# Converting 64-bit weights with a scaled float copy and a sign factor, and spreading the routing of a fused attention and expert kernel over three steps

## The chip, the cores and the metric

The kernel runs on one core of a Trainium2 chip. Its engines are TensorE (PE), VectorE (DVE), ScalarE (ACT), GpSimd (POOL) and SyncE (SP), which here only issues DMAs. Each engine runs its own instructions in the order in which they were issued, and waits on semaphores for the others. The metric is device time in microseconds (us), lower is better.

## The reference

Three layers follow one another:

```python
def phi(x):                                   # q, k, v: 4 x 8 heads x 576 x 64
    proj = x @ w_phi                          # 64 -> 128
    proj = proj - max(abs(proj), axis=-1)
    return concat([exp(proj), exp(-proj)])
kv = phi(k).T @ v;  z = phi(k).sum(tokens)
attn = (phi(q) @ kv) / (phi(q) @ z + 1e-6)    # 2304 tokens x 512
logits = attn @ w_gate                        # 8 experts
e = argmax(logits);  g = softmax(logits)[e]
y = g * (relu(attn @ w1[e]) @ w2[e])          # in order of tokens, up to 576 rows an expert
h = y @ w_in                                  # 512 -> 2048
out = (h - tanh(h)) @ w_out                   # 2048 -> 512
```

All inputs are float32, apart from `w_in` and `w_out`, which arrive as 64-bit floats (the division by sqrt makes them so) and are converted on the chip.

## The kernel before, in words

The first 235 us are attention, routing and weight conversion together; then come the experts and the last layer, unit by unit, almost wholly matmuls.

**Attention** runs in steps `s` over 18 chunks of 128 tokens (`for s in range(NCH + LAG + 2)`). A step works on the keys of chunk `s`, the queries of chunk `s - 5` (`proj("q", j)`) and the numerators of chunk `s - 6` (`num`). TensorE's order in a step: project the keys (L301), transpose the older queries (L377), sum key features times values of the chunk before (L343), project the queries (L301), numerators (L415), gates (L330). Both projections go through the same PSUM tile `xb`, so each of them waits until VectorE has read out the other one: `sub` takes a maximum (L309) and subtracts it (L312). A step is here reckoned from the start of its key projection to that of the next: step 9 begins at 65.89 us, step 18, the first without keys, at 171.84 us.

**Conversion.** A weight is two 32-bit words, `lo` and `hi`. Steps 5 to 17 convert one piece each of 128 x 1024 weights (8 of `w_in`, 5 of `w_out`): `cv_load` fetches the raw piece (two buffers, 1 MB) two steps ahead, `cv_main` runs `cv_bits` on VectorE: three integer instructions put the float together (L86, L89, L92), a fourth (L95) makes a 0/1 mask from the square that ScalarE takes of `hi` (L102, `cv_mask`), and GpSimd multiplies by it (L97). A step later `cv_hi` (ScalarE, L272) rounds the result to the high part and `cv_lo` (GpSimd, L275) subtracts for the low part. Six more pieces of 512 columns (`late_bits`) are converted inside the first expert unit.

**Routing** goes by groups of three chunks. When a group's last numerators are there (its `since` is 0), `route1` runs 14 short VectorE instructions (L443 to L484): gates, argmax, softmax weight. A step later TensorE counts ranks (`prefix`, L504 to L507) and VectorE runs `route2` and `table` (L516 to L560). Another step later TensorE adds the group to the slot table (`map_mm`, L578) and VectorE adds it up (`map_add`, L585). For the first three groups ScalarE then scales one chunk per step (`xscale`, L436) and SyncE stores it; for the others GpSimd scales all three at once (L491). `weave` deals these short instructions out on VectorE behind the query's `sub`.

What sets the order is the order of the calls in the step loop; each engine keeps it.

Of the kernel before, what the change touches and what calls it, by code (L numbers as in the profile page):

```python
# [8 lines left out]
F32 = mybir.dt.float32  # L9
F32R = mybir.dt.float32r  # L10
BF16 = mybir.dt.bfloat16
I32 = mybir.dt.int32
AF = mybir.ActivationFunctionType
ALU = mybir.AluOpType
AX = mybir.AxisListType

P = 128
# [20 lines left out]
def build(nc, tc, ctx, qT, kT, vT, v, w_phi, w_gate, w12, win, wout, out, cap):  # L38
# [7 lines left out]
    const = ctx.enter_context(tc.tile_pool(name="const", bufs=1))  # L46
# [13 lines left out]
    ident = const.tile([P, P], F32, name="ident")  # L60
    reg1 = const.tile([1, 1], I32, name="reg1")
    reg = const.tile([1, E], I32, name="reg")
    sq_b = const.tile([P, 2], F32, name="sq_b")
    ids = [const.tile([P, 6], I32, name=f"ids{i}") for i in range(2)]

    NS = 6 * U
    idt = const.tile([P, NS], mybir.dt.int16, name="idt")
    few = const.tile([P, 3 * E + 2], F32, name="few")
    srt, wu, uk, e1off = few[:, 0:E], few[:, E:2 * E], few[:, 2 * E:3 * E], few[:, 3 * E:]
    reg1f = e1off[:, 1:2]  # L70
# [10 lines left out]

    NP = 512

    def cv_bits(t, a, m):
        lo, hi = t[:, :, 0], t[:, :, 1]
        nc.vector.tensor_scalar(out=a, in0=hi, scalar1=3, scalar2=0x3FFFFFFF,  # L86
                                op0=ALU.logical_shift_left, op1=ALU.bitwise_and)
        yield
        nc.vector.scalar_tensor_tensor(out=a, in0=lo, scalar=29, in1=a,  # L89
                                       op0=ALU.logical_shift_right, op1=ALU.bitwise_or)  # L90
        yield
        nc.vector.scalar_tensor_tensor(out=a, in0=hi, scalar=-0x40000000, in1=a,  # L92
                                       op0=ALU.bitwise_and, op1=ALU.bitwise_or)
        yield
        nc.vector.tensor_scalar(out=m, in0=m, scalar1=1.0, scalar2=None, op0=ALU.is_ge)  # L95
        af = a.bitcast(F32)
        nc.gpsimd.tensor_tensor(out=af, in0=af, in1=m, op=ALU.mult)  # L97
        yield

    def cv_mask(t, m):  # L100

        nc.scalar.activation(out=m, in_=t[:, :, 1].bitcast(F32), func=AF.Square, scale=2.0 ** 15 / 1.125)  # L102

    def cv_split(af, fh, fl):
        nc.scalar.copy(fh, af)
# [21 lines left out]
    def attention():  # L127
# [14 lines left out]
        cv = stk.enter_context(tc.tile_pool(name="cv", bufs=2, side="right"))  # L142
# [35 lines left out]
            out=tri, in_=ones, compare_op=ALU.is_gt, fill=0.0, base=0,  # L178
# [70 lines left out]
        for src, dh, dl, n in ((win, w_in_h, w_in_l, 4 * FF2), (wout, w_oa_h, w_oa_l, NOA * DM)):  # L249
            fh = dh.rearrange("p a b -> p (a b)")  # L250
            fl = dl.rearrange("p a b -> p (a b)")
            for o in range(0, n, NPC):
                pieces.append((src, fh[:, o:o + NPC], fl[:, o:o + NPC], o))
        raw, cvw, cvm = {}, {}, {}
        NRAW = 2

        def cv_load(i):
            if i < len(pieces):
                raw[i] = cv.tile([P, NPC, 2], I32, tag="raw", name="raw", bufs=NRAW)
                cv_fetch(raw[i], pieces[i][0], pieces[i][3], NPC)  # L260

        def cv_m(i):
            cv_mask(raw.pop(i), cvm.pop(i))

        def cv_main(i):
            a = cv.tile([P, NPC], I32, tag="a", name="a")
            cvw[i] = a.bitcast(F32)
            cvm[i] = cv.tile([P, NPC], BF16, tag="m", name="m")
            yield from cv_bits(raw[i], a, cvm[i])

        def cv_hi(i):
            nc.scalar.copy(pieces[i][1], cvw[i])  # L272

        def cv_lo(i):
            nc.gpsimd.tensor_tensor(out=pieces[i][2], in0=cvw.pop(i), in1=pieces[i][1].bitcast(F32), op=ALU.subtract)  # L275
# [41 lines left out]
        def kexp(i):  # L317
            t = kd.pop(("k", i))
            e = kp_p.tile([P, H, 2, DF], F32, tag="kp", name="kp")
            nc.scalar.activation(out=e[:, :, 0, :], in_=t, func=AF.Exp)  # L320
            nc.scalar.activation(out=e[:, :, 1, :], in_=t, func=AF.Exp, scale=-1.0)
            kp[i] = e

# [65 lines left out]
        early = groups[:3]  # L389
        xq, late = [], []  # L390
        GM = max(map(len, groups))
        dls, rs, rt, tab, ohu = {}, {}, {}, {}, {}
# [241 lines left out]
        CV = {s: s - LAG for s in range(LAG, LAG + len(pieces))}  # L634
# [10 lines left out]
        maps = groups[:-2]  # L645
# [9 lines left out]
        def flush():  # L655
            while late:
                late.pop(0)()

        for s in range(NCH + LAG + 2):
            i, j, jt = s, s - LAG, s - LAG - 1  # L660
            jn = jt if s < SD else jt - 1 if s > SD else -1
            kk, qq, tt = i < NCH, 0 <= j < NCH, 0 <= jt < NCH
            pc, pd = CV.get(s), CV.get(s - 1)
            since = {cs: s - (cs[-1] + LAG + 1 + (cs[-1] + LAG + 1 >= SD)) for cs in groups}
            scaled = xq[:1]
            del xq[:1]
            stores = list(scaled)
            if s == SK:
                stk.close()
                mo["alloc"]()  # L670
                qpools.append(st.enter_context(tc.tile_pool(name="qp2", bufs=1)))
            if kk:
                proj("k", i, xb if i > LAG or i % 2 == 0 else yb)
            if tt:
                trans(jt)
                qexp(jt, 0)
                qexp(jt, 1)
            if jn == NCH - 2:
                first_gather()
            for cs in maps:  # L680
                if since[cs] == 1:
                    prefix(cs)
            if 0 <= i - 1 < NCH:
                kv_step(i - 1)
            if pd is not None:
                cv_hi(pd)
                cv_lo(pd)
            if kk:
                for _ in sub("k", i):
                    pass  # L690
            bits = iter(()) if pc is None else cv_main(pc)
            for _ in itertools.islice(bits, 2):
                pass
            if qq:
                proj("q", j, xb)
            if i - 1 in strad:
                kv_second(i - 1)
            if kk:
                kexp(i)
            if qq:  # L700
                for _ in sub("q", j):
                    pass
            for _ in itertools.islice(bits, 1):
                pass
            if 0 <= jn < NCH:
                num(jn)
            if kk:
                vgate(i)
            if pc is not None:
                cv_m(pc)  # L710
            smalls = []
            for cs in groups:
                if since[cs] == 0 and cs != tailg[1]:
                    smalls.append(route1(cs))
                    stores += cs if cs in maps and cs not in early else ()
                if since[cs] == 1 and cs in maps:
                    smalls.append(itertools.chain(route2(cs), table(cs)))
                if since[cs] == 2 and cs in maps[:-1]:
                    map_mm(cs)
                    smalls.append(map_add(cs))  # L720
            weave([], smalls)
            for _ in bits:
                pass
            flush()
            for c in scaled:
                xscale(c)
# [44 lines left out]
        if G == 1:  # L771
# [7 lines left out]
                                           op0=ALU.not_equal, op1=ALU.mult)  # L779
# [4 lines left out]
                                    op0=ALU.min)  # L784
# [3 lines left out]
    def experts():  # L788
# [243 lines left out]
        def late_bits(f):  # L1032
            a, m = late_tiles(f)
            for t, lo, hi in late_parts(f):
                cv_mask(t, m[:, lo:hi])
            for t, lo, hi in late_parts(f):
                yield from cv_bits(t, a[:, lo:hi], m[:, lo:hi])

# [252 lines left out]
```

## Time and profile before

| | us |
|---|---|
| three runs | 724.57, 728.09, 728.88; median 728.09 |
| profiled execution | 729.03, of which the span (first to last instruction) is 727.1 |
| busy: TensorE / VectorE / ScalarE / GpSimd | 666.5 / 550.1 / 430.1 / 242.5 |

The span is in microseconds from its first instruction. Busy counts instructions that run, also while they are held up inside. A matmul's mean granted clock was 0.971 of full speed. In the view by windows, the columns are: the stretch, its length, then for PE, PEld (weight load), DVE, ACT and POOL the busy time and in brackets the number of instructions, the granted TensorE clock, the busy share of the DMA engines and GB/s.

### The profile page before, as it was taken

The numbers are of one execution on the slowest core, as the hardware profiler recorded it, in microseconds if no ns is written. First come the engines' busy times: TensorE is split into PE (matmuls) and PEld (weight loads), VectorE is DVE, ScalarE is ACT, GpSimd is POOL, SyncE is SP. The second block draws the span as 40 slices with busy tenths as digits, with TensorE's granted clock in tenths as the row PEclk, the third lists the DMA queues.
The fourth block names the chain that finished last, engine by engine and source line by source line (L and its number), as shares of the span: only waits on it lengthen the run. The fifth ranks groups of instructions, "written<-read, shape, count | busy, mean of one in ns | idle before, by whom it ended". The sixth has DMA issues, their size and how long they took to land.

```text
span 727.1 us, 17580 instructions
## 1 busy us (share of the span) xinstructions
PE 666.5 (92%) x7148; PEld 645.7 (89%) x7148; DVE 550.1 (76%) x871; ACT 430.1 (59%) x786; POOL 242.5 (33%) x211
## 2 busy tenths in 40 slices
PE   8898787978777999999999999999999999999995
PEld 6787676867665999999999999999999999999985
DVE  3789989997676687998896663887896654787983
ACT  2476876876445465666765554666765454666661
POOL 1044543444140224256263011243362011243451
PEclk9999999989897999999999999999999999999997
DMA  5988684772343664011021452000132551000211
GB/s 151 285 246 270 204 267 155 241 227 92 85 141 117 197 206 132 1 51 55 17 90 48 150 171 91 1 12 23 41 91 63 161 166 43 1 23 13 67 35 37
DMA packets 59755, 81.21 MB, mean 112 GB/s; under 512 B 23392, under 2 KB 32736, under 8 KB 58000
## 3 DMA queue, kind: packets, MB, share of 16 engines
q1 hardware_dynamic: 56336, 71.84, 31.6%
q0 software_dynamic: 2624, 8.06, 3.9%
q8 instruction: 58, 0.95, 0.5%
q14 instruction: 33, 0.27, 0.1%
q10 hardware_dynamic: 704, 0.08, 0.1%
HBM read 66.99 MB, written 12.98 MB: 110 GB/s over the span
## 4 chain that ended last, share of the span: by engine, by line
PE 57%; DVE 10%; DMA 7%; issue 4%; ACT 3%; POOL 1%; POOLq 0%; DVEq 0%; ACTq 0%; SPq 0%
PE h L848 9%; PE h L849 9%; PE h L850 9%; PE acc L848 8%; PE acc L849 8%; PE acc L850 8%; DMA out<-row,ids 6%; DVE y L938 1%; DVE al L917 1%; PE kvb L343 1%; DVE y L936 1%; PE kvb L629 1%; PE h L867 1%; DVE th L940 1%; DMA row<-xs,ids 1%
## 5 line engine op out<-in xcount | busy, mean ns | idle before, releaser
L929 POOL TENSOR_SCALAR al<-ut 128x576 fp32r<-128x576 f32 (+1 forms) x51 | 84.7, 1660 | 148.7 <-ACT ut L925 64.1
L848 PE MATMUL h<-xh,w_in_h 128*128 128x288 f32 x384 | 115.0, 299 | 0.7 <-ACT ut L925 0.7
L849 PE MATMUL h<-xl,w_in_h 128*128 128x288 f32 x384 | 114.5, 298 | 0.0
L850 PE MATMUL h<-xh,w_in_l 128*128 128x288 f32 x384 | 114.1, 297 | 0.0
L835 DVE TENSOR_TENSOR w<-raw,w 128x512 fp32r<-128x512 f32 x98 | 69.4, 725 | 39.9 <-ACT w L830 37.7
L830 ACT CAST w<-raw 128x512 fp32r<-128x512 f32 x98 | 59.1, 620 | 54.3 <-DMA raw<-w 22.3
L924 ACT COPY hs<-h 128x576 f32<-128x576 f32 (+1 forms) x51 | 31.3, 613 | 97.0 <-PE h L850 58.7
L848 PEld LDWEIGHTS h<-xh,w_in_h 128*128 128x128 f32 x384 | 72.5, 189 | 0.9 <-ACT ut L925 0.9
L849 PEld LDWEIGHTS h<-xl,w_in_h 128*128 128x128 f32 x384 | 72.3, 188 | 0.0
L850 PEld LDWEIGHTS h<-xh,w_in_l 128*128 128x128 f32 x384 | 72.2, 188 | 0.0
L849 PE MATMUL acc<-al,w_oa_h 128*128 128x288 f32 x240 | 71.0, 296 | 0.9 <-DVE al L917 0.9
L848 PE MATMUL acc<-ah,w_oa_h 128*128 128x288 f32 x240 | 71.0, 296 | 0.0
L850 PE MATMUL acc<-ah,w_oa_l 128*128 128x288 f32 x240 | 70.7, 295 | 0.0
L969 POOL DMA_INDIRECT out<-row,ids x18 | 22.9, 1271 | 127.5 <-DVE row L967 115.0
L917 DVE TENSOR_TENSOR al<-y,ah 128x576 fp32r<-128x576 f32 (+1 forms) x51 | 40.0, 784 | 33.3 <-ACT ah L916 30.2
L309 DVE TENSOR_REDUCE m<-xb 128x8 f32<-128x1024 f32 x33 | 40.1, 1216 | 25.0 <-PE xb L301 25.0
L848 PE MATMUL h<-xh,w 128*128 128x288 f32 x192 | 58.6, 305 | 0.1
L849 PE MATMUL h<-xl,w 128*128 128x288 f32 x192 | 57.4, 299 | 0.0
L850 PE MATMUL h<-xh,w 128*128 128x288 f32 x192 | 57.3, 298 | 0.0
L848 PE MATMUL acc<-ah,w 128*128 128x288 f32 x192 | 56.9, 296 | 0.0
L849 PE MATMUL acc<-al,w 128*128 128x288 f32 x192 | 56.6, 295 | 0.0
L850 PE MATMUL acc<-ah,w 128*128 128x288 f32 x192 | 56.5, 294 | 0.0
(222 smaller groups left out, 1918.2 us busy)
## 6 DMA issues: line engine op xcount, KB each, us to landing
raw<-w SPq DMA_DIRECT2D x98, 256.0 KB, 2.9
raw<-win SPq DMA_DIRECT2D x8, 1024.0 KB
raw<-wout SPq DMA_DIRECT2D x5, 1024.0 KB, 5.1
k<-kT SPq DMA_DIRECT2D x18, 256.0 KB, 4.5
vt<-vT SPq DMA_DIRECT2D x18, 256.0 KB, 4.4
q<-qT SPq DMA_DIRECT2D x18, 256.0 KB, 3.4
out<-zero SPq DMA_DIRECT2D x18, 256.0 KB, 7.3
v<-v SPq DMA_DIRECT2D x16, 256.0 KB
```

What stands on the lines that cost most here:

```text
L309: nc.vector.tensor_reduce(out=m, in_=ps, axis=AX.X, op=ALU.max, apply_absolute_value=True)
L343: nc.tensor.matmul(kvb[64 * a:64 * a + 64, bank, col * NKV:col * NKV + VS], kp[i][:, 4 * g + hp, s, 64 * a:64 * a + 64], vt[:, 2 * hp + g, :],
L629: nc.tensor.matmul(acc[d][:, 0:BLK], xt[c][:, d * P:(d + 1) * P], ohu[c], start=False, stop=(c == NCH - 1), skip_group_check=True)
L830: nc.scalar.copy(d[:, 0], t)
L835: eng.tensor_tensor(out=d[:, 1], in0=t, in1=d[:, 0].bitcast(F32), op=ALU.subtract)
L848: nc.tensor.matmul(o, ah, bh, start=first, stop=False, skip_group_check=True)
L849: nc.tensor.matmul(o, ah, bl, start=False, stop=False, skip_group_check=True)
L850: nc.tensor.matmul(o, al, bh, start=False, stop=last, skip_group_check=True)
L917: nc.vector.tensor_tensor(out=AL[a][:, i], in0=y2[:, i], in1=AH[a][:, i].bitcast(F32), op=ALU.subtract)
L924: nc.scalar.copy(hs[:, i], h[:, i, 0:BLK])
L929: nc.gpsimd.tensor_scalar(out=AL[a][:, i], in0=ut[:, i], scalar1=C2, scalar2=None, op0=ALU.is_gt)
L969: ins = nc.gpsimd.indirect_dma_start(out=out[:, :], out_offset=bass.IndirectOffsetOnAxis(ap=ids[j % 2][0:RCH, rc:rc + 1], axis=0), in_=r[0 ...
```

## The change

Three things change.

1. **Conversion.** ScalarE now starts it: `cv_size` copies `hi`, read as a float, times 2^-112 into `a`. VectorE then makes a factor of +1 or -1 from the top 16 bits of the weight (`m`, an int16 instruction that reads every fourth half word), shifts `a` left by 3 and joins `lo`; GpSimd multiplies by the factor. `cv_mag` runs at the end of the step before the piece's own step.
2. **Cast of the old piece.** `cv_hi` and `cv_lo` move from before the key's `sub` to between the two exponentials of the keys, which became two parts of `kexp`.
3. **Routing** of the first four groups: `route1` runs five parts in one step and the rest in the next; `prefix`, `route2`, `table` and then `map_mm`, `map_add` come one step later.

```diff
+    def cv_size(t, a):
+        nc.scalar.activation(out=a.bitcast(F32), in_=t[:, :, 1].bitcast(F32), func=AF.Copy, scale=2.0 ** -112)
     def cv_bits(t, a, m):
-        lo, hi = t[:, :, 0], t[:, :, 1]
-        nc.vector.tensor_scalar(out=a, in0=hi, scalar1=3, scalar2=0x3FFFFFFF,
-                                op0=ALU.logical_shift_left, op1=ALU.bitwise_and)
+        top = t.rearrange("p n w -> p (n w)").bitcast(I16).rearrange("p (n w) -> p n w", w=4)[:, :, 3]
+        nc.vector.tensor_scalar(out=m.bitcast(I16), in0=top, scalar1=-0x8000, scalar2=0x3F80,
+                                op0=ALU.bitwise_and, op1=ALU.bitwise_or)
         yield
-        nc.vector.scalar_tensor_tensor(out=a, in0=lo, scalar=29, in1=a,
+        nc.vector.tensor_scalar(out=a, in0=a, scalar1=3, scalar2=None, op0=ALU.logical_shift_left)
+        yield
+        nc.vector.scalar_tensor_tensor(out=a, in0=t[:, :, 0], scalar=29, in1=a,
                                        op0=ALU.logical_shift_right, op1=ALU.bitwise_or)
         yield
-        nc.vector.scalar_tensor_tensor(out=a, in0=hi, scalar=-0x40000000, in1=a,
-                                       op0=ALU.bitwise_and, op1=ALU.bitwise_or)
-        yield
-        nc.vector.tensor_scalar(out=m, in0=m, scalar1=1.0, scalar2=None, op0=ALU.is_ge)
         af = a.bitcast(F32)
         nc.gpsimd.tensor_tensor(out=af, in0=af, in1=m, op=ALU.mult)
-    def cv_mask(t, m):
-        nc.scalar.activation(out=m, in_=t[:, :, 1].bitcast(F32), func=AF.Square, scale=2.0 ** 15 / 1.125)
...
+        paced = groups[:4]
...
             for cs in maps:
-                if since[cs] == 1:
+                if since[cs] == 1 + (cs in paced):
                     prefix(cs)
             if 0 <= i - 1 < NCH:
                 kv_step(i - 1)
-            if pd is not None:
-                cv_hi(pd)
-                cv_lo(pd)
...
-            if kk:
-                kexp(i)
+            ke = kexp(i) if kk else iter(())
+            next(ke, None)
+            if pd is not None:
+                cv_hi(pd)
+                cv_lo(pd)
+            for _ in ke:
+                pass
             if qq:
                 for _ in sub("q", j):
                     pass
-            for _ in itertools.islice(bits, 1):
-                pass
...
-            if pc is not None:
-                cv_m(pc)
+            if CV.get(s + 1) is not None:
+                cv_mag(CV[s + 1])
             smalls = []
             for cs in groups:
+                slow = int(cs in paced)
                 if since[cs] == 0 and cs != tailg[1]:
-                    smalls.append(route1(cs))
+                    rgen[cs] = route1(cs)
+                    smalls.append(itertools.islice(rgen[cs], 5) if slow else rgen[cs])
+                if slow and since[cs] == 1:
+                    smalls.append(rgen[cs])
...
-                if since[cs] == 1 and cs in maps:
+                if since[cs] == 1 + slow and cs in maps:
                     smalls.append(itertools.chain(route2(cs), table(cs)))
-                if since[cs] == 2 and cs in maps[:-1]:
+                if since[cs] == 2 + slow and cs in maps[:-1]:
                     map_mm(cs)
                     smalls.append(map_add(cs))
             weave([], smalls)
             for _ in bits:
                 pass
...
         def late_bits(f):
             a, m = late_tiles(f)
             for t, lo, hi in late_parts(f):
-                cv_mask(t, m[:, lo:hi])
+                cv_size(t, a[:, lo:hi])
```

VectorE in the second half of step 8, where the first group's routing begins, before:

```order
L86 TENSOR_SCALAR a<-raw 128x1024
L89 SCALAR_TENSOR_TENSOR a<-raw,a 128x1024
L309 TENSOR_REDUCE m<-xb 128x8
L312 TENSOR_TENSOR d<-xb,m 128x1024
L92 SCALAR_TENSOR_TENSOR a<-raw,a 128x1024
L443 TENSOR_SCALAR r<-dl 128x24
L444 RECIPROCAL r<-r 128x24
L453 TENSOR_TENSOR lgx<-dl,r 128x192
L457 TENSOR_REDUCE lg<-lgx 128x24
L460 TENSOR_REDUCE mx<-lg 128x3
L463 TENSOR_TENSOR ls<-lg,mx 128x24
L467 TENSOR_TENSOR cand<-lg,mx 128x24
```

and with the change:

```order
L93 TENSOR_SCALAR m<-raw 128x1024
L96 TENSOR_SCALAR a<-a 128x1024
L311 TENSOR_REDUCE m<-xb 128x8
L314 TENSOR_TENSOR d<-xb,m 128x1024
L448 TENSOR_SCALAR r<-dl 128x24
L449 RECIPROCAL r<-r 128x24
L458 TENSOR_TENSOR lgx<-dl,r 128x192
L462 TENSOR_REDUCE lg<-lgx 128x24
L465 TENSOR_REDUCE mx<-lg 128x3
L468 TENSOR_TENSOR ls<-lg,mx 128x24
L98 SCALAR_TENSOR_TENSOR a<-raw,a 128x1024
```

Before, seven more short ones and L95 follow; now the six short ones stand alone, the instruction with two inputs from SBUF (L98) stands last, and nothing long stands between the query's L314 and the short ones.

ScalarE in step 16 before:

```order
L383 ACTIVATE qp<-yb 128x1024 x2
L272 CAST w_oa_h<-a 128x1024
L320 ACTIVATE kp<-d 128x8x128
L321 ACTIVATE kp<-d 128x8x128
L425 COPY dl<-yb 128x72
L427 COPY x<-yb 128x2x4x64
L334 COPY v_154<-sb 128x8x8
L102 ACTIVATE m<-raw 128x1024
L436 ACTIVATE x<-x,r 128x64 x8
```

and with the change:

```order
L386 ACTIVATE qp<-yb 128x1024 x2
L322 ACTIVATE kp<-d 128x8x128
L274 CAST w_oa_h<-a 128x1024
L324 ACTIVATE kp<-d 128x8x128
L430 COPY dl<-yb 128x72
L432 COPY x<-yb 128x2x4x64
L337 COPY v_154<-sb 128x8x8
L87 ACTIVATE a<-raw 128x1024
L441 ACTIVATE x<-x,r 128x64 x8
```

The cast moved behind the first key exponential, and L87 belongs to the next step's piece, where L102 belonged to this one's.

TensorE from step 18's transposes to step 19's, before:

```order
L377 MATMUL yb<-ident,d 128x128 x8
L504 MATMUL sb<-oh,tri 128x24
L506 MATMUL sb<-oh,ones 128x16
L506 MATMUL sb<-oh,ones 128x8
L507 MATMUL sb<-cum,ones 128x24
L343 MATMUL kvb<-v_155,kp 64x74 x32
L301 MATMUL xb<-wphi,q 128x128 x8
L415 MATMUL kvb<-kvs_163,qp 64x74 x32
L377 MATMUL yb<-ident,d 128x128 x8
```

and with the change:

```order
L380 MATMUL yb<-ident,d 128x128 x8
L346 MATMUL kvb<-v_155,kp 64x74 x32
L303 MATMUL xb<-wphi,q 128x128 x8
L420 MATMUL kvb<-kvs_163,qp 64x74 x32
L380 MATMUL yb<-ident,d 128x128 x8
```

The fourth group's rank counts (L504, now L509) follow a step later, and its slot table after step 20's numerators instead of after step 19's query projection.

## Rows read from the trace of the kernel before

**Rows 1.** Windows: steps 5-8, 9-17, 18-20, first expert stretch

```profile
30.38:65.89 35.51, 32.26 (x732) 29.72 (x729) 31.17 (x31) 24.94 (x36) 15.09 (x8) 1.00 0.89 278
65.89:171.84 105.95, 83.54 (x1746) 76.64 (x1742) 98.95 (x147) 79.24 (x158) 47.34 (x32) 0.94 0.66 205
171.84:195.03 23.19, 16.43 (x271) 14.72 (x271) 15.35 (x32) 11.73 (x23) 8.80 (x9) 0.85 0.42 124
234.80:330.00 95.20, 94.32 (x696) 93.58 (x696) 78.96 (x132) 52.82 (x95) 33.62 (x27) 0.98 0.38 118
```

**Rows 2.** Windows: step 10 alone

```profile
77.23:90.07 12.84, 8.56 (x188) 7.77 (x188) 12.50 (x18) 11.11 (x26) 5.14 (x3) 1.00 0.65 207
```

**Rows 3.** Waits, steps 9-17: total us, times, longest

```profile
PE xb L301 <- DVE d L312: 16.7, 12, 2.5
DVE m L309 <- PE xb L301: 3.7, 3, 1.8
```

**Rows 4.** DVE by line, steps 9-17: busy us, mean ns, idle before

```profile
L312 DVE TENSOR_TENSOR d<-xb,m 128x1024 f32<-128x1024 f32 x18 | 22.0, 1224 | 0.6
L309 DVE TENSOR_REDUCE m<-xb 128x8 f32<-128x1024 f32 x18 | 21.8, 1213 | 3.7 <-PE xb L301 3.7
L89 DVE SCALAR_TENSOR_TENSOR a<-raw,a 128x1024 int32<-128x1024 int32 x9 | 19.5, 2166 | 0.3
L95 DVE TENSOR_SCALAR m<-m 128x1024 bf16<-128x1024 bf16 x9 | 3.8, 419 | 0.0
```

**Rows 5.** Users of tile raw, 30-180 us: ns min/median/max, starts, forms

```profile
L86 DVE TENSOR_SCALAR a<-raw x13: 682/684/1087, 34.1 to 165.1; 128x1024 int32<-128x1024 int32 x13
L89 DVE SCALAR_TENSOR_TENSOR a<-raw,a x13: 1224/1225/3399, 34.8 to 165.8; 128x1024 int32<-128x1024 int32 x13
L92 DVE SCALAR_TENSOR_TENSOR a<-raw,a x13: 1212/1215/2027, 38.3 to 171.2; 128x1024 int32<-128x1024 int32 x13
...
DMA to landing us min/median/max: 5.0/5.1/5.1
```

**Rows 6.** Timeline, step 10: start us, us, instruction, idle before, releaser

```profile
84.16 2.38 POOL L275 TENSOR_TENSOR w_in_l<-a,w_in_h 128x1024 fp32r<-128x1024 f32 x1 [0.52 <-ACT w_in_h L272]
84.23 3.40 DVE L89 SCALAR_TENSOR_TENSOR a<-raw,a 128x1024 int32<-128x1024 int32 x1
```

**Rows 7.** ACT by line, steps 9-17

```profile
L320 ACT ACTIVATE kp<-d 128x1024 f32<-128x1024 f32 x9 | 9.5, 1058 | 2.1 <-issue 1.5 <-ACT w_oa_h L272 0.3 <-ACT w_in_h L272 0.3
...
L272 ACT CAST w_oa_h<-a 128x1024 fp32r<-128x1024 f32 x4 | 4.2, 1054 | 1.1 <-POOL a L97 1.0
```

**Rows 8.** Timeline: two routing parts and the long instruction behind each

```profile
100.73 0.18 DVE L443 TENSOR_SCALAR r<-dl 128x24 f32<-128x24 f32 x1
...
102.51 0.17 DVE L467 TENSOR_TENSOR cand<-lg,mx 128x24 f32<-128x24 f32 x1
...
103.98 0.42 DVE L95 TENSOR_SCALAR m<-m 128x1024 bf16<-128x1024 bf16 x1
...
148.67 0.17 DVE L516 TENSOR_TENSOR pos<-sb,oh 128x24 f32<-128x24 f32 x1
...
150.83 0.42 DVE L95 TENSOR_SCALAR m<-m 128x1024 bf16<-128x1024 bf16 x1
```

**Rows 9.** Timeline, step 10: from the numerators to the slot table

```profile
84.34 2.32 PE L415 MATMUL yb<-kvs,qp 128*64 128x74 f32 x64
...
86.70 0.22 ACT L425 COPY dl<-yb 128x72 f32<-128x72 f32 x1 [0.70 <-PE yb L415]
...
87.58 0.34 PE L578 MATMUL sb<-tb,ta 128*96 128x98 bf16 x3 [0.50 <-ACT v L334]
```

**Rows 10.** Timeline, TensorE in steps 18 to 20

```profile
175.02 0.19 PE L504 MATMUL sb<-oh,tri 128*128 128x24 bf16 x1 [2.09 <-DVE oh L474]
...
182.65 1.16 PE L301 MATMUL xb<-wphi,q 64*128 64x128 f32 x16
...
188.02 1.94 PE L377 MATMUL yb<-ident,d 128*128 128x128 f32 x8 [2.15 <-DVE d L312]
```

More of the change, by code (lines that the diff above doesn't have):

```diff
@@ L12 @@
 I32 = mybir.dt.int32
+I16 = mybir.dt.int16
 AF = mybir.ActivationFunctionType
@@ L66, in build @@
     NS = 6 * U
-    idt = const.tile([P, NS], mybir.dt.int16, name="idt")
+    idt = const.tile([P, NS], I16, name="idt")
     few = const.tile([P, 3 * E + 2], F32, name="few")
@@ L82, in build @@
     NP = 512
+    def cv_size(t, a):
+        nc.scalar.activation(out=a.bitcast(F32), in_=t[:, :, 1].bitcast(F32), func=AF.Copy, scale=2.0 ** -112)
     def cv_bits(t, a, m):
-        lo, hi = t[:, :, 0], t[:, :, 1]
-        nc.vector.tensor_scalar(out=a, in0=hi, scalar1=3, scalar2=0x3FFFFFFF,
-                                op0=ALU.logical_shift_left, op1=ALU.bitwise_and)
+        n = a.shape[-1]
+        top = t.rearrange("p n w -> p (n w)").bitcast(I16).rearrange("p (n w) -> p n w", w=4)[:, :, 3]
+        nc.vector.tensor_scalar(out=m.bitcast(I16), in0=top, scalar1=-0x8000, scalar2=0x3F80,
+                                op0=ALU.bitwise_and, op1=ALU.bitwise_or)
         yield
-        nc.vector.scalar_tensor_tensor(out=a, in0=lo, scalar=29, in1=a,
+        nc.vector.tensor_scalar(out=a, in0=a, scalar1=3, scalar2=None, op0=ALU.logical_shift_left)
+        yield
+        nc.vector.scalar_tensor_tensor(out=a, in0=t[:, :, 0], scalar=29, in1=a,
                                        op0=ALU.logical_shift_right, op1=ALU.bitwise_or)
         yield
-        nc.vector.scalar_tensor_tensor(out=a, in0=hi, scalar=-0x40000000, in1=a,
-                                       op0=ALU.bitwise_and, op1=ALU.bitwise_or)
-        yield
-        nc.vector.tensor_scalar(out=m, in0=m, scalar1=1.0, scalar2=None, op0=ALU.is_ge)
         af = a.bitcast(F32)
@@ L253, in attention @@
                 pieces.append((src, fh[:, o:o + NPC], fl[:, o:o + NPC], o))
-        raw, cvw, cvm = {}, {}, {}
+        raw, cvw, cva = {}, {}, {}
         NRAW = 2
@@ L260, in cv_load, with cv_mag @@
                 cv_fetch(raw[i], pieces[i][0], pieces[i][3], NPC)
-        def cv_m(i):
-            cv_mask(raw.pop(i), cvm.pop(i))
+        def cv_mag(i):
+            if i in raw:
+                a = cva[i] = cv.tile([P, NPC], I32, tag="a", name="a")
+                cvw[i] = a.bitcast(F32)
+                cv_size(raw[i], a)
         def cv_main(i):
[L266 to L269, printed above, removed]
+            m = cv.tile([P, NPC], BF16, tag="m", name="m")
+            yield from cv_bits(raw.pop(i), cva.pop(i), m)
         def cv_hi(i):
@@ L320, in kexp @@
             nc.scalar.activation(out=e[:, :, 0, :], in_=t, func=AF.Exp)
+            yield
             nc.scalar.activation(out=e[:, :, 1, :], in_=t, func=AF.Exp, scale=-1.0)
@@ L389, in attention @@
         early = groups[:3]
+        paced = groups[:4]
+        rgen = {}
         xq, late = [], []
@@ L708, in attention @@
                 vgate(i)
-            if pc is not None:
-                cv_m(pc)
+            if CV.get(s + 1) is not None:
+                cv_mag(CV[s + 1])
             smalls = []
             for cs in groups:
+                slow = int(cs in paced)
                 if since[cs] == 0 and cs != tailg[1]:
-                    smalls.append(route1(cs))
+                    rgen[cs] = route1(cs)
+                    smalls.append(itertools.islice(rgen[cs], 5) if slow else rgen[cs])
+                if slow and since[cs] == 1:
+                    smalls.append(rgen[cs])
+                if since[cs] == slow:
                     stores += cs if cs in maps and cs not in early else ()
-                if since[cs] == 1 and cs in maps:
+                if since[cs] == 1 + slow and cs in maps:
                     smalls.append(itertools.chain(route2(cs), table(cs)))
-                if since[cs] == 2 and cs in maps[:-1]:
+                if since[cs] == 2 + slow and cs in maps[:-1]:
                     map_mm(cs)
```

## The prediction, on record before the changed kernel ran

> **What bounds the kernel now.** I read the windows first, then the waits, then VectorE's lines and the timeline.
>
> From 234.8 us on TensorE is busy 94.32 of 95.20 us [rows 1]: the experts run without gaps, so whatever the first stage saves arrives at the end, and the six late pieces, beside gapless matmuls, save nothing. The stage to look at is steps 9 to 17: 105.95 us, VectorE busy 98.95, TensorE 83.54, ScalarE 79.24. Step 10 shows it best: VectorE busy 12.50 of 12.84, TensorE 8.56 [rows 2]. The waits say the same: 16.7 us of TensorE's waiting before its projections is for VectorE's subtraction, which frees the shared tile; only 3.7 us go the other way [rows 3]. So each of these nine steps is as long as VectorE's queue. Steps 5 to 8 are not: 8.9 us each, TensorE and VectorE about equal and the DMA engines at 0.89 [rows 1].
>
> VectorE's queue has one more thing in it. L89 takes 1.225 us in most steps, but its mean in steps 9 to 17 is 2.166, its longest 3.399 [rows 4, 5]. In step 10 GpSimd's subtraction of the old piece starts at 84.16 and takes 2.38; L89 starts 0.07 later and ends 1.1 us after it [rows 6]. An instruction with two inputs from SBUF thus stands until the GpSimd one is through. That costs 9 x (2.166 - 1.225) = 8.5 us here.
>
> **The change, part by part** (on the profiled execution, 729.03 us; the median of the runs is 0.94 lower).
>
> *VectorE's instructions per piece.* Before: 0.684 + 1.225 + 1.215 + 0.419 = 3.54 us [rows 4, 5]. After: the join 1.225, the shift 0.684 (it is L86 with a closer input), and the 16-bit sign instruction, which the trace doesn't have. Its nearest row is L86: one input, same step of 8 bytes, 0.684. Ends: 0.419 if 16 bits are as good here as in L95, 1.22 if it runs like L89. I take 0.684: sum 2.59, 0.95 less. The Trainium skill ("VectorE: DVE Perf Modes", What auto-detection actually checks) asks step 1 of 16-bit data before two are packed, and lets one SBUF input still go two per cycle; by it the price is L86's, not L95's, which would make the sum 2.4 lower over nine steps. In the nine bound steps: 9 x 0.95 = **-8.6 us**. ScalarE's copy stands for its square at the same size.
>
> *GpSimd and the cast.* The cast now follows the first key exponential, which needs the key's subtraction. From the end of that subtraction: exponential 1.06, cast 1.05 [rows 7], so GpSimd's subtraction runs from 2.1 to 4.5 us. VectorE meanwhile: sign and shift 1.37 (GpSimd's multiplication, begun after the last join, should be through), then the query's L309 and L312, 2.44 [rows 4], which read PSUM; at 3.8 it comes to the short ones or the join and stands up to 0.7 us. 9 x 0.7 = 6 us in place of 8.5: **-2.5**. Ends: no holding at all, -8.5; held a whole 2.38 in each step, +13.
>
> *VectorE's waits for TensorE.* 3.7 us [rows 3], after stretches where TensorE had stood still (its granted clock there is 0.94 in the mean, [rows 1]). With shorter stalls I take half away: **-1.9** (0 to -3.7).
>
> *Routing.* In the nine steps its instructions are the same but for one L585; spreading moves them. Parts: 1.78, 1.47 and 2.16 us [rows 8], before 3.25 and 2.16 in two of three steps. As VectorE bounds all three steps either way, evening out gives nothing by itself. A cover goes: L585 had L92 in front of it while TensorE made its input. Now it comes at 3.8 us after the key's subtraction, while its input needs query projection 1.16 [rows 10], numerators 2.32, then 1.22 from the first copy to the end of the slot table [rows 9]: 4.7. It waits 0.9, of which 0.7 would have been spent standing for GpSimd anyway: 3 x 0.2 = **+0.7** (0 to 2.7). Each key projection after a slot table starts that much later too; but VectorE comes to its result only after L585, six short ones and a join, 3 us, so nobody waits.
>
> *Steps 18 to 20* (23.19 us, TensorE busy 16.43, [rows 1]). The fourth group's counts leave step 18, and with them TensorE's wait of 2.09 for routing. From step 19's query projection (182.65) to the next transposes (188.02) there are 5.37 us, as the query's maximum had to queue behind the group's table. Now the table stands behind it: 1.16 + 2.44 + about 0.1 = 3.7. Together 2.09 + 1.67 = **-3.8** [rows 10]. GpSimd's scaling of that group, its three stores on SyncE's queue and one `xscale` on ScalarE move into step 18, which had room: 11.73 and 8.80 busy of 23.19. Ends: -2 and -6 (with TensorE at its full clock, here 0.85).
>
> *Steps 5 to 8.* VectorE loses 0.95 per step, but TensorE and the DMAs are as full: **-0.7** (0 to -2.2).
>
> *ScalarE's new waits.* L87 stands at the end of a step before the scaling of tokens and the next query exponentials. It waits for the raw piece, whose load goes out when the join two pieces earlier is done, some 3.4 us into the same step, and takes 5.1 [rows 5]: 8.5 us. ScalarE is there about 10 us in (numerators, two copies). It also waits for GpSimd's subtraction to free `a`, at about the same time. 0 us, with 1.5 us to spare; what it costs when that is gone is the third rival. On SyncE's queue the raw load stays before `vt`, `v` and the stores; they already waited there for L92 or ScalarE's square.
>
> Sum: -8.6 - 2.5 - 1.9 + 0.7 - 3.8 - 0.7 = -16.8; 729.03 - 16.8 = **712 us**. Steps 9 to 17 come to 93.7, or 10.4 each, still above TensorE's 8.56.
>
> **The rivals.**
>
> *The holding-up only moves.* GpSimd's subtraction, now late in the step, may catch the short instructions or the join in all nine steps instead of four, each for 2.38: 21.4 against 6, so 712 + 15 = **727**. For it: it now always ends near where VectorE needs the port, and the sign and shift can be held as well (L86 once took 1.09, [rows 5]). Against: it starts 1.7 us before VectorE gets there. It decides if the cast slips by about 1.7 us, as when ScalarE is late with the query exponentials. The Trainium skill ("SBUF — State Buffer", SBUF: two separate sides) has this as its rule: whoever takes the shared ports first keeps them for the whole instruction, one-input instructions at double rate included. L89 behind L275 agrees.
>
> *The 16-bit instruction runs at L89's pace*: 13 x 0.54 = 7 us at most, **719**.
>
> *ScalarE becomes the chain (slower).* If the raw piece lands late, L87 holds the scaling, the next query exponentials and through them the numerators in every conversion step. The slack is 1.5 us; past a landing of 6.6 each further us costs up to 13. To lose 7 us against now, 24 must be spent: a landing of 8.5. At 8.8 it would be **740**. For it: the DMA share of 0.89 in steps 5 to 8. Against: 5.0 to 5.1 in the landings shown, and 0.66 in steps 9 to 17, where steps of 10.4 us make it 0.75.
>
> *It does not stop at VectorE's queue.* If neither GpSimd nor TensorE holds VectorE, a further 6 + 1.9 go: **704**.
>
> That the order isn't what the text says is out: the rows of the change show it.
>
> **How the numbers follow.** Forecast, 705 to 719 with its own unknowns: 0.62. The slow 16-bit instruction, 717 to 722: 0.12. Holding-up moves, 721 to 730: 0.14. Slower: 0.06. Better than forecast, 700 to 705: 0.06. The range reaches from 703 to 724, which leaves out the slower case, half of the moved one and some of the best. A change of 1% (7.3 us, below 720.8 or above 735.4) is about what a measurement can tell. Faster 0.79, same 0.15, slower 0.06.
>
> **What would show it.** VectorE: 13 sign instructions near 0.68, 13 shifts near 0.68, 13 joins at 1.22 with few above 2; L92's and L95's time gone. Steps 9 to 17 near 94 us, with VectorE still at over 90% busy. TensorE's wait for the routing before its counts gone from step 18, and steps 18 to 20 under 20 us. No wait of ScalarE's L87 on a raw load. It would be wrong if the join's mean, or that of the short ones before it, stayed near 2 us, if L87 waited for DMA, or if TensorE and not VectorE ended the waits at the projections.

## The result, and the profile after

The changed kernel takes 715.44 us (median; 715.09 to 719.08) against 728.0 for the one before on the same chip: a ratio of 0.9847, 95% interval 0.9803 to 0.9892. It is 1.5% faster, with the whole interval under 1, and 3.4 us above the 712 of the forecast. Its profiled execution took 715.38 with a span of 713.5, 13.6 less than before. The windows say where; their columns are those of [rows 1].

```profile
29.30:62.91 33.61, 32.13 (x732) 29.72 (x728) 29.23 (x28) 26.61 (x37) 13.02 (x8) 1.00 0.92 281
62.91:163.40 100.49, 79.97 (x1745) 74.52 (x1742) 85.07 (x136) 77.99 (x151) 46.94 (x33) 0.97 0.69 218
163.40:184.14 20.74, 16.05 (x275) 14.51 (x273) 15.79 (x31) 12.21 (x30) 8.79 (x9) 0.84 0.48 152
222.00:317.00 95.00, 95.00 (x698) 94.51 (x698) 75.41 (x125) 53.62 (x96) 32.58 (x27) 0.97 0.38 120
```

Steps 5 to 8 are 1.9 us shorter, 9 to 17 5.5, 18 to 20 2.5; the experts still run without gaps. The other 3.8 lie before step 5, between step 20 and the experts, and in the experts. In the profiled runs below, where these places hold nearly the same work, they come out up to 2.7, 5.0 and 2.4 apart, so none of it is put down to the change. In the middle one, where 1.8 of the 3.8 lie, TensorE's busy time and granted clock differ, not its work (before, then after):

```profile
195.04:234.67 39.63, 28.86 (x380) 24.44 (x378) 25.67 (x97) 20.63 (x54) 10.71 (x19) 0.87 0.33 108
```

```profile
184.14:221.97 37.83, 27.15 (x381) 23.26 (x379) 25.67 (x98) 20.48 (x54) 10.73 (x19) 0.93 0.35 113
```

Steps 9 to 17 are the surprise. VectorE's busy time fell by 13.9 us, from 98.95 to 85.07, more than the 11.1 that were forecast, yet the nine steps became only 5.5 shorter: VectorE now idles 15.4 us of them, where it idled 7.0. Its lines in the nine steps (busy us, mean ns, idle before):

```profile
L311 DVE TENSOR_REDUCE m<-xb 128x8 f32<-128x1024 f32 x18 | 21.9, 1215 | 0.5 <-PE xb L303 0.2
L98 DVE SCALAR_TENSOR_TENSOR a<-raw,a 128x1024 int32<-128x1024 int32 x9 | 11.0, 1218 | 0.0
L93 DVE TENSOR_SCALAR m<-raw 128x1024 int16<-128x1024 int16 x9 | 7.3, 816 | 0.0
L96 DVE TENSOR_SCALAR a<-a 128x1024 int32<-128x1024 int32 x9 | 6.2, 684 | 0.0
L472 DVE TENSOR_TENSOR cand<-lg,mx 128x24 f32<-128x24 f32 x3 | 3.0, 1016 | 0.0
...
L448 DVE TENSOR_SCALAR r<-dl 128x24 f32<-128x24 f32 x3 | 1.3, 417 | 0.0
```

The join is no longer held up (1218 ns, against 2166 in [rows 4]); what GpSimd holds now are the sign instruction and short ones: 9 x 0.13, 3 x 0.84, 3 x 0.24, together 4.4 us (a sole L472 takes 0.17 [rows 8]). One such holding, at the end of step 9:

```profile
71.15 2.37 POOL L277 TENSOR_TENSOR w_in_l<-a,w_in_h 128x1024 fp32r<-128x1024 f32 x1 [2.35 <-ACT w_in_h L274]
...
72.65 0.91 DVE L472 TENSOR_TENSOR cand<-lg,mx 128x24 f32<-128x24 f32 x1
```

The waits of the nine steps (total, times, longest) show who holds whom:

```profile
PE xb L303 <- DVE d L314: 18.1, 9, 2.5
...
DVE pos L521 <- ACT v L337: 5.1, 3, 2.4
DVE idc L590 <- PE sb L583: 3.7, 1, 3.7
DVE mx L482 <- ACT ls L470: 1.9, 3, 0.7
DVE idc L588 <- PE sb L583: 0.8, 1, 0.8
...
DVE m L311 <- PE xb L303: 0.2, 1, 0.2
```

TensorE waits for VectorE's subtraction as long as in [rows 3], 18.1 us against 16.7. VectorE's waits for the projections are gone (3.7 to 0.2), but 11.5 us of others stand in their place: for ScalarE's copy of the value gates (`pos` reads the same PSUM tile, `sb`, and the program makes it wait for that copy), for the slot table, for the routing's exponential. Before, L92 filled the time until the gate copy was done.

By step, two stand out (step 10, then 14):

```profile
72.80:84.57 11.77, 9.80 (x192) 9.23 (x189) 9.16 (x15) 6.99 (x11) 6.51 (x6) 0.86 0.80 255
...
118.36:132.42 14.06, 10.55 (x256) 9.83 (x252) 9.45 (x16) 10.54 (x23) 5.26 (x5) 1.00 0.64 205
```

Step 10 ran at a granted clock of 0.86, as did step 13. The timeline of TensorE there:

```profile
79.25 1.28 PE L303 MATMUL xb<-wphi,q 64*128 64x128 f32 x16 [1.97 <-DVE d L314]
80.47 3.75 PE L420 MATMUL yb<-kvs,qp 128*64 128x74 f32 x64
```

After 1.97 us of waiting for VectorE the numerators took 3.75 us instead of 2.32 [rows 9]: part of them ran at the lower of the two levels, 1.2 instead of 2.4 GHz. Step 14, whose chunk straddles two batches, has no low clock. There the key exponentials wait 3.1 us for the second sum, and the cast behind the first now delays all that ScalarE does after it, up to the gate copy and the slot table (L590's 3.7).

The users of the raw piece answer to [rows 5]:

```profile
L87 ACT ACTIVATE a<-raw x13: 1145/1167/1182, 31.4 to 153.3; 128x1024 f32<-128x1024 f32 x13
...
  POOL w_oa_l L277: 1.6, 3
  POOL w_in_l L277: 1.6, 6
...
DMA to landing us min/median/max: 5.0/5.0/5.0
```

L87 waits for GpSimd alone, never for a load. In steps 18 to 20 the answer to [rows 10] is:

```profile
173.12 0.17 PE L509 MATMUL sb<-oh,tri 128*128 128x24 bf16 x1 [1.69 <-DVE oh L479]
...
173.30 1.16 PE L303 MATMUL xb<-wphi,q 64*128 64x128 f32 x16
...
177.13 1.94 PE L380 MATMUL yb<-ident,d 128*128 128x128 f32 x8 [2.67 <-DVE pos L521]
```

Step 18 became 2.9 us shorter (6.94), but step 19 0.4 longer: the wait for the routing moved there with the counts (1.69), and from the projection to the next transposes it is 3.83 instead of 5.37. What makes the counts wait is GpSimd's last subtraction, which holds one short routing instruction ahead of them for 2.23 us instead of 0.18:

```profile
170.22 2.38 POOL L277 TENSOR_TENSOR w_oa_l<-a,w_oa_h 128x1024 fp32r<-128x1024 f32 x1 [1.16 <-ACT w_oa_h L274]
...
170.41 2.23 DVE L474 TENSOR_TENSOR cand<-cand,e 128x24 f32<-128x24 f32 x1
```

### The profile page after: what moved, and what is told of

It is laid out like the page before. It is cut to its first block, busy times and chain, and to the rows that moved or that the text cites. A ratio compares the mean times of both kernels' runs of the same rounds, so it can differ in the third digit from the quotient of the medians.

```text
span 713.5 us, 17559 instructions
## 1 busy us (share of the span) xinstructions
PE 658.2 (92%) x7148; PEld 639.7 (90%) x7148; DVE 530.9 (74%) x850; ACT 431.7 (60%) x786; POOL 238.8 (33%) x211
## 4 chain that ended last, share of the span: by engine, by line
PE 66%; DVE 15%; DMA 8%; ACT 6%; issue 3%; POOL 2%; ACTq 0%; POOLq 0%; DVEq 0%
PE h L858 9%; PE h L859 9%; PE h L860 9%; PE acc L858 8%; PE acc L859 8%; PE acc L860 8%; DMA out<-row,ids 6%; PE kvb L346 4%; PE xb L303 3%; PE yb L420 3%; DVE d L314 2%; DVE m L311 2%; DVE a L98 1%; DVE y L948 1%; DVE al L927 1%
## 5 line engine op out<-in xcount | busy, mean ns | idle before, releaser
L927 DVE TENSOR_TENSOR al<-y,ah 128x576 fp32r<-128x576 f32 (+1 forms) x51 | 38.8, 760 | 34.5 <-ACT ah L926 31.9
```

The lines of the kernel that those rows point to most:

```text
L927: nc.vector.tensor_tensor(out=AL[a][:, i], in0=y2[:, i], in1=AH[a][:, i].bitcast(F32), op=ALU.subtract)
```

## The experiments

Lengths are in us and come from one profiled execution each; the ratio, over several runs, is to the kernel before on the same chip. "Low" names the steps of 9 to 17 with a granted clock under 0.9; a low step is some 1.7 us longer (e9 below), so differences of that size between single executions can be the clock's.

| kernel | ratio, interval | 5-8 | 9-17 | 18-20 | low |
|---|---|---|---|---|---|
| before | 1 | 35.5 | 105.9 | 23.2 | 11, 13, 17 |
| the change | 0.9847, 0.9803-0.9892 | 33.6 | 100.5 | 20.7 | 10, 13 |
| e1 conversion only | 0.9845, 0.9817-0.9874 | 33.8 | 95.9 | 24.0 | 13 |
| e2 no spreading | 0.9916, 0.9889-0.9944 | 33.8 | 100.4 | 25.0 | 10, 13, 15 |
| e3 old place of the cast | 0.9818, 0.9794-0.9842 | 34.4 | 99.6 | 20.6 | 11, 17 |
| e4 spreading only | 0.9891, 0.9858-0.9924 | 34.9 | 102.0 | 21.8 | 14 |
| e5 gates first | 0.9880, 0.9858-0.9902 | 33.4 | 103.7 | 20.6 | 10, 12, 13, 15 |
| e6 sign twice | 0.9854, 0.9824-0.9884 | 33.9 | 97.7 | 20.4 | 15 |
| e7 shift late | 0.9904, 0.9883-0.9924 | 34.5 | 101.1 | 20.1 | 12 |
| e8 gates first, copy late | 0.9764, 0.9743-0.9785 | 34.1 | 95.7 | 19.6 | 12, 15 |
| e9 dummies | 0.9852, 0.9836-0.9867 | 37.7 | 96.8 | 21.1 | none |
| e10 fourth group only | 0.9818, 0.9801-0.9835 | 34.5 | 95.3 | 19.4 | 13 |
| e11 e8, old place of the cast | 0.9745, 0.9716-0.9773 | 35.0 | 91.2 | 19.5 | 12 |
| e12 e11, dummies | 0.9768, 0.9737-0.9800 | 34.8 | 93.6 | 20.5 | 13 |

Against what was expected, with the ratio times 728.0: e3 (714.8), e6 (717.4) and e8 (710.8) came out at or near theory A, e1 (716.7) at the total of theory B. For e2 (721.9), e4 (720.1), e5 (719.3) and e7 (721.0) no theory named the number that came. The others are taken up below.

### The three parts of the change

**e1, conversion only**: `paced` empty, the cast in its old place.

```diff
-        paced = groups[:4]
+        paced = groups[:0]
...
+            if pd is not None:
+                cv_hi(pd)
+                cv_lo(pd)
             if kk:
                 for _ in sub("k", i):
...
-            ke = kexp(i) if kk else iter(())
-            next(ke, None)
-            if pd is not None:
-                cv_hi(pd)
-                cv_lo(pd)
-            for _ in ke:
-                pass
+            if kk:
+                for _ in kexp(i):
+                    pass
```

> The new conversion alone; cast and routing as before the change. Theory A (in the changed kernel steps 9 to 17 are a ring of waits: key subtraction, query projection, numerators, ScalarE's copies, short routing instructions, join, key subtraction; VectorE is not the only bound any more): about 719 us, VectorE loses some 13 us of busy time, but its waits for TensorE and ScalarE grow from 4 to about 10 us in the nine steps. Theory B (VectorE's queue alone sets the steps, and the parts add up): 717, that is 728 less 8.6 and less what L89's holding-up cost.

**e2, no spreading**: the first line of that alone.

> The change without the spread routing (conversion and moved cast). A: 717 to 719; in nine steps the spreading is worth little, since each step goes round the same ring, but steps 18 to 20 lose the 2.5 us that they gained. B: 718, 2.5 to 4 us behind the change, all of it in steps 18 to 20.

**e3, the old place of the cast**: the rest of it alone.

> The change with the cast of the old piece back in its first place. A: 714 to 716: the sign and shift are held up by GpSimd's subtraction in about four steps, some 2 us each, but they have slack before the query projection ends; step 14 gets back about 1 us since the cast no longer stands between the two exponentials there. B: 719 to 721, since every microsecond of holding-up counts.

**e4, spreading only**: the kernel before, with the change's lines on `paced` and `slow`.

> The kernel before with the routing spread over three steps and nothing else. Both: steps 9 to 17 stay at about 106 us since VectorE bounds them in either order, steps 18 to 20 gain 2 to 4: 724 to 726. If spreading were what made the change faster: 718 or less.

The conversion alone (e1) has the whole gain. Spreading alone gains about 1.1%, conversion 1.6, both (e3) 1.8: they overlap. The moved cast adds nothing to that: without spreading it makes the kernel slower (e1 to e2, intervals apart), with it the two can't be told apart (e3 and the change). The nine steps of e1, and VectorE's line for the shift, held 0.49 us each time:

```profile
61.51:157.36 95.85, 78.86 (x1745) 72.56 (x1741) 86.22 (x139) 79.04 (x157) 47.09 (x32) 0.98 0.72 227
```

```profile
L96 DVE TENSOR_SCALAR a<-a 128x1024 int32<-128x1024 int32 x9 | 10.5, 1170 | 0.0
```

VectorE is 1.2 us busier there than in the changed kernel, and the steps are 4.6 shorter. In the old place of the cast the join is past GpSimd's subtraction as well, as the shift takes the holding-up, 4.4 us in all (the sign 0.8 more, the short ones none): the gain forecast for moving the cast came from the new order of the conversion's instructions. The Trainium skill ("SBUF — State Buffer", SBUF: two separate sides) says that a one-input instruction at double rate is shut out too; the shift agrees, 1170 ns instead of 684.

Spreading shortens steps 18 to 20, as forecast (e1, then e3):

```profile
157.36:181.38 24.02, 18.19 (x271) 16.42 (x271) 15.32 (x30) 10.85 (x22) 9.65 (x9) 0.79 0.38 121
```

```profile
162.87:183.51 20.64, 15.96 (x275) 14.42 (x273) 15.81 (x31) 12.20 (x30) 8.77 (x9) 0.83 0.49 153
```

In steps 9 to 17, where next to nothing was forecast for it, its sign differs: 3.9 us shorter on the old conversion (before to e4), 3.7 longer on the new one (e1 to e3), no difference with the moved cast (e2 to the change). Much of that is where the low clock fell: e4 has two low steps fewer than the kernel before, and e3 one more than e1. Step 14, into which spreading moves a slot table, is 1.9 of e3's 3.7 (12.34 us against 10.47 in e1).

### Does VectorE's queue set the steps?

**e6, the sign twice**: VectorE repeats the sign instruction, about 0.69 us more a piece.

```diff
+        nc.vector.tensor_scalar(out=m.bitcast(I16), in0=top, scalar1=-0x8000, scalar2=0x3F80,
+                                op0=ALU.bitwise_and, op1=ALU.bitwise_or)
         yield
         nc.vector.tensor_scalar(out=a, in0=a, scalar1=3, scalar2=None, op0=ALU.logical_shift_left)
```

> The change with the sign instruction issued twice, 0.684 us more for VectorE in each of 13 steps (8.9 in all, 6.2 in steps 9 to 17). A: a third of it shows, 717 to 719, since in most steps VectorE waits afterwards anyway. B: 721 to 724, all of it in the nine bound steps and part of it in the others.

```profile
62.48:160.14 97.66, 78.77 (x1743) 72.84 (x1741) 89.23 (x145) 78.21 (x152) 47.14 (x33) 0.98 0.71 223
```

```profile
L95 DVE TENSOR_SCALAR m<-raw 128x1024 int16<-128x1024 int16 x9 | 6.3, 695 | 0.3
```

The second sign takes 6.3 us in the nine steps, and the kernel takes as long as the change (0.9854 against 0.9847). VectorE's busy time rises by 4.2 only, largely as the short ones are held up less, and its idle time is 8.4 instead of 15.4: the added work fills its waits. The nine steps did not grow; they are 2.8 us shorter, with one low step fewer. The theory that VectorE's queue alone sets these steps falls.

**e7, the shift late**: the shift behind the query's subtraction.

```diff
-            for _ in itertools.islice(bits, 2):
+            for _ in itertools.islice(bits, 1):
                 pass
...
                 for _ in sub("q", j):
                     pass
+            for _ in itertools.islice(bits, 1):
+                pass
```

> The change with the shift moved behind the query's subtraction, where L92 stood before the change. VectorE's work is the same. A: the shift covers 0.68 us of the waits of L521, L588 and L590, and the query's subtraction starts when its projection ends: 712 to 714. B: 715, no change.

```profile
L96 DVE TENSOR_SCALAR a<-a 128x1024 int32<-128x1024 int32 x10 | 13.9, 1392 | 0.0
```

The shift is now held 0.7 us each time, and the kernel is slower than the change, 0.9904 against 0.9847 (the intervals overlap by 0.001). Whether the holding-up is why is not shown: of the 5.9 us by which its profiled execution is longer, 0.6 lie in the nine steps and 3.9 between step 20 and the experts, where the granted clock was 0.80 instead of 0.93.

### VectorE's new waits

**e5, gates first**: the value gates ahead of the numerators on TensorE and ScalarE, so that `pos` finds the copy done.

```diff
-            if 0 <= jn < NCH:
-                num(jn)
             if kk:
                 vgate(i)
+            if 0 <= jn < NCH:
+                num(jn)
```

> The change with the gate matmuls ahead of the numerators, so that ScalarE copies the gates before it copies the numerators. VectorE's L521 waits for that copy (5.1 us in three steps), and the slot table, on which L588 and L590 wait (4.5 us), needs it too. A: these waits fall to under 3 us in all and the time to about 711. B (VectorE's work sets the step): 715, no change.

**e8**: the same, and ScalarE's scaled copy behind the routing.

```diff
-            if CV.get(s + 1) is not None:
-                cv_mag(CV[s + 1])
             smalls = []
...
             weave([], smalls)
+            if CV.get(s + 1) is not None:
+                cv_mag(CV[s + 1])
```

> Gates first and, beside that, ScalarE's scaled copy of the next piece behind the routing's exponential instead of ahead of it. A: L482's wait for that exponential (1.9 us in three steps) goes too: about 1 us under the run with the gates first alone, 710. B: 715.

TensorE's numerators in e5's step 12, and ScalarE's wait for numerators in its nine steps (6.4 in the change):

```profile
104.19 4.11 PE L420 MATMUL yb<-kvs,qp 128*64 128x74 f32 x64
```

```profile
ACT dl L430 <- PE yb L420: 14.7, 8, 3.7
```

VectorE's wait for the routing's exponential, e5, then e8:

```profile
DVE mx L482 <- ACT ls L470: 6.2, 3, 3.6
```

```profile
DVE mx L482 <- ACT ls L470: 2.0, 2, 1.1
```

In e5 the wait for the gate copy is gone, but the gain is lost again. Four steps are low, two of them at 0.76 and 0.75; the numerators come later, and the exponential, which ScalarE runs behind its copies of them and behind the scaled copy, comes later with them. In e8 the scaled copy (1.2 us) is out of the way, and two steps are low, as in the change; the kernel is 0.9764, below the change with the intervals apart, and its nine steps are 4.8 us shorter. How much of e5's loss was the copy and how much the clock is open. VectorE waits for the exponential as long in e8 as in the change (2.0 against 1.9), but no longer for the gate copy (5.1 in the change). So part of the missing gain had become VectorE's waits for ScalarE.

**e11**: e8 with the cast in its old place.

> Edit: the changed kernel with the value gates ahead of the numerators on TensorE, the scaled copy behind the routing's exponential on ScalarE, and the cast in its old place. Theory M (the moved cast costs by itself, 715.44 against 713.53 without it, and the two other edits are worth 5.0 us on top): 708 to 709, steps 9 to 17 at 94 to 95. Rival (the moved cast cost only because ScalarE's queue had the gate copy, the cast and the scaled copy late in the step, which the two other edits already mend): 710 to 711, steps 9 to 17 at 95.5 to 96.5. If the old place now delays ScalarE's exponentials for the key again with nothing to win: 712 to 714.

0.9745: its profiled execution went beyond theory M (703.65, steps 9 to 17 at 91.2), but its five runs lie between 703.65 and 711.04 with the median at 710.45, which fits the rival. It can't be told apart from e8; the two have the lowest ratios here.

### The granted clock

**e9, dummies**: twelve matmuls that nothing reads ahead of the query projection. The edit put them into steps 5 to 8 as well, which the expectation overlooked.

```diff
+        def warm_sb(n):
+            z = zero.bitcast(BF16)
+            for _ in range(n):
+                nc.tensor.matmul(sb[:, 256:512], z[:, 0:P], z, start=True, stop=True, skip_group_check=True)
...
+            if pc is not None:
+                warm_sb(12)
             if qq:
                 proj("q", j, xb)
```

> Edit: the changed kernel with twelve dummy matmuls on TensorE (128 x 256, bf16, zeros, into a part of a PSUM bank that nothing reads) just ahead of the query projection of each of the nine conversion steps, where TensorE stands waiting for VectorE's subtraction (18.1 us in nine waits, the longest 2.5). At the full clock twelve of them should take some 1.3 us, less than the mean wait of 2.0, so that they cost little by themselves. Theory C (a part of these steps' length is TensorE's low clock, which follows the long waits: steps 10 and 13 ran at 0.86): granted clock 1.00 in all nine steps, steps 10 and 13 shorter by 1 to 2 us each, steps 9 to 17 together 97 to 98.5 instead of 100.5, the kernel 712 to 713.5. Theory W (the low clock is only a sign that TensorE had nothing to do, the steps are set by the waits themselves): the clock rises as well, but steps 9 to 17 stay at 100 to 101 and the kernel at 715 to 717, or up to 9 x 1.3 = 12 us slower if the dummies do not fit into the waits.

Steps 5 to 8 together, then 10, 12 and 13:

```profile
30.12:67.83 37.71, 37.02 (x780) 33.72 (x776) 27.85 (x28) 26.15 (x37) 13.82 (x8) 1.00 0.85 264
```

```profile
77.33:87.33 10.00, 9.66 (x205) 8.87 (x201) 8.96 (x15) 6.98 (x11) 5.57 (x6) 1.00 0.71 228
...
98.31:108.73 10.42, 9.57 (x198) 8.65 (x197) 9.73 (x16) 8.06 (x16) 3.77 (x2) 1.00 0.86 286
108.73:119.53 10.80, 9.66 (x205) 8.87 (x201) 9.67 (x16) 8.79 (x19) 5.06 (x6) 1.00 0.67 206
```

The clock is 1.00 in all nine, steps 10 and 13 are 1.8 and 1.6 us shorter than in the changed kernel, and six of the others (step 12: 10.42 both times) agree within 0.02; step 9 is 0.4 shorter. So each low step had cost some 1.7. The kernel gains nothing overall (0.9852): in steps 5 to 8, where TensorE has no such wait, the dummies cost 4.1, as much as the 3.7 that steps 9 to 17 win.

**e12**: e11 with six dummies, in steps 9 to 17 alone.

> Edit: the kernel with the value gates first, the scaled copy late and the cast in its old place, with six dummy matmuls on TensorE ahead of the query projection in steps 9 to 17 alone (in steps 5 to 8, where TensorE had no wait of that length, twelve of them made each step 0.7 to 1.4 us longer). Its waits there are 0.9 to 1.5 us and one of 2.3, in step 12, which ran at 0.86. Theory C (the low clock follows the long wait and makes that step longer; where it falls differs from run to run, which is why the runs without dummies lie between 703.7 and 711.0 us): granted clock 1.00 in steps 9 to 17, step 12 some 1.5 us shorter (10.9 instead of 12.4), the nine steps 89 to 90.5, the runs closer together and their median 702 to 706. Rival W (six dummies, some 0.65 us a step, move the projection behind them in steps whose waits are about as short, and the clock elsewhere decides the spread): steps 9 to 17 at 91 to 94, the median 709 to 713.

Steps 12 and 13, and TensorE at the start of step 13:

```profile
93.39:105.83 12.44, 9.40 (x193) 8.24 (x191) 11.81 (x16) 10.31 (x22) 4.84 (x2) 1.00 0.87 291
105.83:116.32 10.49, 10.49 (x194) 9.63 (x194) 8.92 (x17) 7.05 (x15) 5.06 (x5) 0.84 0.66 206
```

```profile
105.83 1.79 PE L308 MATMUL xb<-wphi,k 64*128 64x128 f32 x16 [1.90 <-DVE d L319]
```

Theory C missed: 0.9768 is no better than e11, and the runs lie from 708.1 to 713.8. The rival's numbers came out (median 710.96, nine steps 93.65). Step 12 has its clock back, but not its length (12.44; 12.42 in e11): there VectorE, busy for 11.81, does set the step. TensorE's wait went to the next key projection, 1.90 us, and the low clock followed it to step 13. Step 15 is 1.3 us longer as well (10.94 against 9.61), at a clock of 1.00; there TensorE stood for 1.78 us within its key projection, and the profile shows no cause.

### Which groups to spread

**e10**: e3 with `paced = groups[3:4]`.

> Edit: the changed kernel with the cast put back in its old place (ahead of the query projection's subtraction, as in the conversion-only kernel) and with only the fourth group's routing spread over three steps; the first three keep two. Theory S (spreading the first three costs time in steps 9 to 17, since conversion alone had 95.9 there and conversion with all four spread 99.6; spreading the fourth is what shortens steps 18 to 20 from 24.0 to 20.6): steps 9 to 17 at 96 to 97.5, steps 18 to 20 at 20.5 to 21.5, the kernel 710.5 to 712. Theory N (the 3.7 us between those two in steps 9 to 17 was the luck of where the low clock fell): steps 9 to 17 at 98.5 to 100, steps 18 to 20 at 20.6, the kernel 713 to 714, as with all four spread.

```profile
64.63:159.92 95.29, 78.98 (x1743) 72.76 (x1741) 84.15 (x139) 78.88 (x158) 47.56 (x32) 0.98 0.71 226
```

The windows are those of theory S, 95.3 and 19.4, but the ratio is that of e3, 0.9818 both times: its profiled execution is longer than e3's before step 5 (1.3) and between step 20 and the experts (2.8, of which 2.1 are TensorE's busy time, at a granted clock of 0.84 instead of 0.92). In the nine steps, then, spreading the first three groups costs something; whether it does in the kernel's time is open.

## Why the prediction was right, and where it failed

- **VectorE's instructions per piece, -8.6**: right as work taken from VectorE. Sign 0.684, shift 0.684, join 1.218, to 0.01 of the prices taken. The Trainium skill ("VectorE: DVE Perf Modes", What auto-detection actually checks) gave the sign L86's price and not L95's; the trace agrees, 684 ns.
- **GpSimd and the cast, -2.5**: the size was better than forecast (4.4 us of holding-up are left, not 6), but the cause was wrong: e1 comes to 5.2 without moving the cast. The move itself costs where routing is not spread (e1 to e2). Step 14 of the change shows ScalarE's later work waiting for the cast, but two more low steps are 3.4 of the 4.6 us between the nine steps of e1 and e2, so that cause is not shown for all of it.
- **VectorE's waits for TensorE, -1.9**: measured -3.5.
- **"So each of these nine steps is as long as VectorE's queue"** is the step that failed, and with it "Steps 9 to 17 come to 93.7" (100.5). It held for step 10 of before, busy 12.50 of 12.84, the step that it was read from. It did not hold for two of them even then: in steps 11 and 17 TensorE, at a low clock, was the busier (below). Once 13.9 us are taken out, VectorE, ScalarE and TensorE wait for one another in turn. e6 shows it: a second sign of 6.3 us on VectorE cost nothing. The check that the prediction named, VectorE at over 90% busy, came out at 85%.

```profile
90.07:99.75 9.68, 9.68 (x184) 9.00 (x184) 8.28 (x10) 5.54 (x9) 4.50 (x2) 0.82 0.78 246
...
160.52:171.84 11.32, 10.93 (x185) 10.08 (x185) 8.83 (x10) 5.99 (x11) 4.49 (x2) 0.73 0.24 72
```

- **The lost cover, +0.7**: mis-sized, and looked for in one place. L588 and L590 wait 4.5 us, L521 5.1 and L482 1.9. Before, L92 ran ahead of each of these places and filled the time.
- **The clock** was read only as a mean of 0.94. At 1.7 us a step, the nine steps would be 3.4 us shorter without it (e9), half of the 6.8 that are missing. The kernel before had three low steps, so the forecast started from a length that held some of this already; what it cost there, no run shows.
- **Steps 18 to 20, -3.8**: -2.5. The projection to the transposes was right (3.83 against 3.7), but the wait for the counts moved to step 19 instead of going: GpSimd's holding-up, which the prediction priced in the nine steps, was put at nothing here and held L474 for some 2 us.
- **Steps 5 to 8, -0.7**: -1.9, inside its ends. **L87** never waited for a load, as forecast; the 16-bit instruction was not slow; the slower rival had nothing to start from.

That the total came out near the forecast is luck: 6.8 us were missing in the nine steps and 1.3 in steps 18 to 20, while steps 5 to 8 gave 1.2 more and 3.8 that no step of it claims went the same way. Of the 3.8, 1.8 lie where the granted clock was higher (0.93 instead of 0.87); what the others are is open.

## What to carry to other kernels

An engine that is 93% busy in the mean need not set the pace in every step, and where it does, it does so only until work is taken from it. Look at the steps one by one. Before pricing a removal at its full length, look at what each remaining instruction would wait for if it came that much earlier, and count as cover every long instruction that goes. Try the parts of a combined change one by one: here one part held the whole gain, and another, added to it alone, made the kernel slower. And when a step is longer than all of its engines' work, look at the granted clock behind its longest TensorE wait before looking for a new dependence.

## What the runs showed of the hardware

- In the changed kernel TensorE waits 1.4 to 2.6 us before each of the nine query projections; the granted clock fell behind two of these waits (1.97 and 2.55 us) and not behind five others of 2.0 to 2.3. So such a wait comes ahead of the low clock, but does not bring it each time, and which steps are hit differs between kernels. With twelve dummies (some 1.5 us) in each wait it stayed at 1.00 in nine steps of nine.
- A GpSimd subtraction of 2.37 us held up VectorE instructions of 24 elements a partition (0.17 to 1.02 us in the mean, and one of 0.18 became 2.23) as well as long ones with one SBUF input (0.684 to 1.39), but not those that read PSUM (1.215 and 1.224 throughout).
